# Fused attention and feed-forward kernel: similarities first, one-hot in steps 2 to 5, value products three key tiles every third step

## The chip, the cores and the metric

The kernel runs on one core of a Trainium2 chip. The core has a matrix engine (TensorE, PE in the profile; its weight loads are listed as PEld), VectorE (DVE), ScalarE (ACT), GpSimd (POOL), and a queue for DMAs (SyncE, SP). The metric is device time in microseconds, the median of several executions; one further execution is profiled.

## What is computed

Three stages, one after the other; the change lies in the first.

```python
# attention, for each batch b (2) and head h (8), 768 rows of 64
q_assign = argmax(q_n @ c_n.T)          # the nearest of 16 centroids of the head
k_assign = argmax(k_n @ c_n.T)
scores = q @ k.T / 8, and -1e9 where q_assign != k_assign
attn = softmax(scores) @ v
# mixing over the rows, then a feed-forward block (512 -> 2048 -> 512)
u = x + (x.T @ U @ V).T
x = u + relu(u @ w_ch1) @ w_ch2
# gated block with a convolution of three rows
h = relu(x @ w_in); gate = sigmoid(conv3(h)); out = (h * gate) @ w_out
```

## The kernel before

**Tiles and steps.** Queries go in tiles of 128 rows, six to a head, 16 heads, so 96 *steps* n (function `step`, L654). Two heads of a batch are a *pair*; there are eight pairs, 0 to 7, of 12 steps each, and s is the step within the pair (`divmod(n, 2 * NT)`). All engines run their own instructions in the order in which the program issues them, so `step` is a schedule written by hand. A step n does, in this order on TensorE:

- `s_mm(n + 2)`: scores of the tile two steps ahead, four matmuls, two of L364 (which finish an earlier `s_mm_ab`) and two of L375. The query and key operands are split in a high and a low part (`ab`, `cd`), and the `cd` tile holds 16 extra rows with the one-hot of the cluster, large where query and key agree. The scores have two PSUM buffers (pool `ps_s`).
- `pv_mm`: value products of the head before (L418), in the steps and with the key tiles that `PLAN` (L651) gives. r counts the steps of a head, shifted by one, so r = 0, 2, 4 are s = 1, 3, 5, 7, 9, 11, two of the six key tiles in each. `fin_t` (L434) turns the finished head back, in s = 1 and 7.
- at times an item of `mixing`, in the steps `MIX_AT` (L652: 0, 4, 8, 10): `mix_t` (L572), six `mix_u` (L588), and `mix_x` (L600) of the first batch, from step 8 of pair 4 on.
- `sims_wide` (s = 2) and `sims_turn` (s = 3), see below.
- `t_mm(n)`: six transposes of the tile's exponentials (L402).

ScalarE and VectorE take what falls due: `t_out(n - 1)` copies the transposed exponentials, one half on each (L409); `s_exp(n + 1)` is the exponential on ScalarE (L393); `s_max(n + 2)` is VectorE's maximum (L381), which the exponential needs. Then come `fin_x` (L440, L443), the evacuation of the mixing item, and `prep(n)` (L620).

**Side work of a pair.** While a pair runs, the next one is prepared: `sims_wide` (L226) multiplies centroids with queries and keys, `sims_copy` (L231, ScalarE) brings the result to SBUF, `sims_turn` (L240) transposes it into the PSUM tile `sim`, five parts on VectorE (`onehot_part`: L257 `mx`, L259 `eq`, L261 `eq` by an index, L263 `m2`, L265 `oh`) make the one-hot, parts 0 and 1 of which read `sim`; `onehot_t` (L273) transposes it, `onehot_rows` (L279, VectorE) scales it to `os`, and four DMAs on SP's queue (L287) put its rows into `cd`. In the pairs from 1 on the parts stand in steps 3, 3, 4, 4, 5 and the last two functions at the end of step 6. For pair 1, prepared during pair 0, there is a form of its own: `sims` (L215), 24 small matmuls ahead of and in step 0, with `warm` matmuls on zeros between them, parts in steps 0, 0, 1, 2, 3, and rows in step 5.

**Other queues.** `load_ops` (L113 to L115, issued by GpSimd) and `load_raw` (L96 to L98, SP) load a pair's operands; `split_ops` (L125, L126, GpSimd) makes the low parts: of the next pair's first head in step 1, of its second in step 7, when its loads have landed. `pump` (steps of odd n) moves the weight jobs on by one operation: with one job to a pair, VectorE's L473, L477 and L481 fall into s = 9, 11 and 1, ScalarE's L468 and L527 into s = 7 and 3.

**The rotating PSUM pool.** `ps_t` has three buffers, all under one tag: the two halves of the transposes of a step, `simw`, `sim`, `oht`, `at` and the mixing tiles take them in turn, so each waits until the tile three before it has been read.

Of the kernel before, what the change touches and what calls it, by code (L numbers as in the profile page):

```python
# [17 lines left out]
F32 = mybir.dt.float32  # L18
# [3 lines left out]
AF = mybir.ActivationFunctionType  # L22
ALU = mybir.AluOpType
# [3 lines left out]
P = 128  # L27
# [6 lines left out]
def tile_kernel(ctx: ExitStack, tc: tile.TileContext, qk, vv, cen, u_w, v_w, w1, w2, win, wout, conv, out):  # L34
    nc = tc.nc
    B, H, D, _, S = qk.shape
    NC = cen.shape[0] // H
# [167 lines left out]

    ohst = {}

    def sims(b, p, tiles=range(NT)):
        rq, rk = raw[b, p]
        if (b, p) not in ohst:  # L210
            ohst[b, p] = {"pm": ps_t.tile([P, NT * 4, NC], F32, tag="t", name="sim")}
        pm = ohst[b, p]["pm"]
        for t in tiles:
            for i, (r, cb) in enumerate(((rq, cbq), (rk, cbk))):
                nc.tensor.matmul(  # L215
                    pm[:, 4 * t + 2 * i:4 * t + 2 * i + 2, :].rearrange("p g c -> p (g c)"),
                    r[:, t * P:(t + 1) * P], cb[:, p], start=True, stop=True,
                )
# [47 lines left out]

    def onehot_t(b, p):
        oh = ohst[b, p]["oh"]
        pair = b * NP + p
        pt = ps_t.tile([4 * NC, S], BF16, tag="t", name="oht")  # L270
        for t in range(NT):
            g0 = 4 * t if pair == 1 else 8 * (t % (NT // 2)) + 4 * (t // (NT // 2))
            nc.tensor.transpose(pt[:, t * P:(t + 1) * P], oh[:, g0:g0 + 4].rearrange("p g c -> p (g c)"), identb)  # L273
        ohst[b, p]["pt"] = pt

    def onehot_rows(b, p):
        pt = ohst.pop((b, p))["pt"]
        os_ = a_oh.tile([4 * NC, S], F32R, tag="os", name="os")
        nc.vector.tensor_scalar(out=os_, in0=pt, scalar1=ohs[:, 0:1], scalar2=ohs[:, 1:2], op0=ALU.mult, op1=ALU.add)  # L279
        put_rows(b, p, os_, range(2))  # L280

    def put_rows(b, p, os_, heads):
# [337 lines left out]
    def prep(n):  # L620

        pair, s = divmod(n, 2 * NT)
        nxt = pair + 1
        if nxt < B * NP:
            b, p = divmod(nxt, NP)
            for part, at in enumerate((3, 3, 4, 4, 5) if nxt > 1 else (0, 0, 1, 2, 3)):
                if s == at and (nxt > 1 or part > 1):
                    sims_onehot(b, p, part)
            if s == 1:
                split_ops(b, p, 0, nc.gpsimd)  # L630
            elif s == 3:
                load_ops(b, p, 1)
            elif s == 7:
                split_ops(b, p, 1, nc.gpsimd)
            elif s == 8:
                load_v(b, p)
            if s == (6 if nxt > 1 else 5):
                onehot_t(b, p)
                onehot_rows(b, p)
        if s == 10 and pair + 2 < B * NP:  # L640
            load_raw(*divmod(pair + 2, NP))
            load_ops(*divmod(pair + 2, NP), 0)
        if n == NQ - 7:
            queue_chunk(1, lambda: wpc)
        if n >= NQ - 7:
            pump(FLOW)
        elif n % 2 == 1 and n > 1:
            pump(THIN)


    PLAN = ({2 * k: (2 * k, 2 * k + 1) for k in range(NK)}, NT - 2), ({k: (2 * k, 2 * k + 1) for k in range(NK)}, NK - 1)  # L651
    MIX_AT = (0, 4, 8, 10)  # L652

    def step(n):  # L654
        pair, s = divmod(n, 2 * NT)
# [4 lines left out]
                mixing.append(mix_t(b))  # L660
                mix_rest(b)
        if n == 0:

            for t in range(2, NT):
                sims(0, 1, (t,))
                warm(1)
        if n + 2 < NQ:
            s_mm(n + 2)

        g, r = divmod(n - NT - 1, NT)  # L670
        ks, last = PLAN[g == NHEAD - 1]
# [6 lines left out]
        elif mixing and (s in MIX_AT or pair == B * NP - 1):  # L678
            mix = mixing.pop(0)
            got = mix[0]()  # L680
        if s == 2 and n < NQ and 1 < pair + 1 < B * NP:
            sims_wide(*divmod(pair + 1, NP))
        if s == 3 and n < NQ and 1 < pair + 1 < B * NP:
            sims_turn(*divmod(pair + 1, NP))
        if 0 <= n < NQ:
            t_mm(n)
        if 0 <= n - 1 < NQ:
# [283 lines left out]
```

## Time and profile before

| | us |
|---|---|
| median of 3 runs | 667.9 (667.74 to 668.18) |
| the profiled execution, device time | 668.33 |
| its span in the profile | 666.3 |
| granted TensorE clock over the span | 1.0 of full speed |

A row of a timeline has the start in us from the span's start, the duration, the engine, the line of the kernel, the operation, and out<-in with partitions x elements; x8 at its end means eight such instructions merged, and the bracket tells the idle time of the engine just before it and what released it. Matmuls are pipelined, so the time from one start to the next is what one costs.

### The profile page before, as it was taken

What the parts mean: (1) busy time and instruction counts of PE and PEld (TensorE: products, weight loads), DVE (VectorE), ACT (ScalarE), POOL (GpSimd) and SP (SyncE); (2) the same over time, 40 slices, a digit from 0 to 9 for tenths busy, and PEclk for the clock granted to TensorE, in tenths of its full rate; (3) what the DMA queues carried; (4) which work ended last, traced back from release to release, by engine and by line L of the source; (5) the groups of instructions that cost most, each with busy time, mean ns of one, the idle gap of its engine ahead of it and who ended that gap; (6) DMA issues with size and microseconds to landing.
All of it is one profiled execution on the core that took longest, in us unless ns stands there. A gap on an engine that the chain in (4) does not pass through costs nothing.

```text
span 666.3 us, 9744 instructions
## 1 busy us (share of the span) xinstructions
PE 648.6 (97%) x3660; PEld 511.5 (77%) x3660; DVE 428.1 (64%) x744; ACT 319.9 (48%) x613; POOL 221.3 (33%) x222
## 2 busy tenths in 40 slices
PE   8999999999999999999999999999999999999997
PEld 6766766666676766789888888888877888888886
DVE  6988788887889875388326868873177445643400
ACT  5765666666666773334213343331135367753511
POOL 3844436252434013046331333331055634321300
PEclk9999999999999999999999999999999999999999
DMA  7765655727273202022102343330013000000111
GB/s 184 147 147 129 140 128 117 173 61 174 60 174 70 91 29 98 1 95 96 65 0 95 105 148 127 126 127 32 1 64 126 1 1 0 3 31 24 41 47 48
DMA packets 19583, 55.45 MB, mean 83 GB/s; under 512 B 3312, under 2 KB 7024, under 8 KB 19536
## 3 DMA queue, kind: packets, MB, share of 16 engines
q1 hardware_dynamic: 15936, 40.08, 20.1%
q0 software_dynamic: 3600, 14.75, 10.9%
q8 instruction: 29, 0.48, 0.3%
q14 instruction: 18, 0.15, 0.1%
HBM read 50.19 MB, written 3.15 MB: 80 GB/s over the span
## 4 chain that ended last, share of the span: by engine, by line
PE 82%; DVE 10%; issue 3%; ACT 2%; POOL 1%; DMA 0%; DVEq 0%; ACTq 0%; POOLq 0%
PE g L860 10%; PE pv L418 9%; PE tr L402 7%; PE h L737 6%; PE h L739 6%; PE h L738 6%; PE a L753 6%; PE a L755 5%; PE a L754 5%; PE sc L364 4%; PE sc L375 4%; PE po L894 3%; PE po L895 3%; PE po L896 3%; DVE e L381 2%
## 5 line engine op out<-in xcount | busy, mean ns | idle before, releaser
L528 POOL TENSOR_TENSOR wl<-wx,wh 128x512 fp32r<-128x512 f32 x48 | 63.1, 1316 | 143.9 <-ACT wh L527 137.9
L393 ACT ACTIVATE e<-sc,nb 128x768 f32<-128x768 f32 x96 | 86.8, 905 | 21.8 <-DVE e L381 21.5
L381 DVE TENSOR_SCALAR_CACHE_REDUCE e<-sc 128x768 f32<-128x768 f32 x96 | 91.3, 952 | 7.2 <-PE sc L375 6.7
L743 DVE SCALAR_TENSOR_TENSOR rl<-h,rh 128x512 fp32r<-128x512 f32 (+1 forms) x52 | 33.7, 647 | 85.8 <-ACT rh L742 85.8
L742 ACT ACTIVATE rh<-h 128x512 fp32r<-128x512 f32 (+1 forms) x52 | 29.3, 563 | 113.1 <-PE h L739 113.1
L402 PEld LDWEIGHTS tr<-identf,e 128*128 128x128 f32 x576 | 65.2, 140 | 23.3 <-issue 5.0
L402 PE MATMUL tr<-identf,e 128*128 128x128 f32 x576 | 81.2, 276 | 1.2 <-ACT tt L581 0.7
L737 PE MATMUL h<-uh,wh 128*128 128x512 f32 (+1 forms) x208 | 78.3, 376 | 1.6 <-DVE rl L743 1.6
L753 PE MATMUL a<-rh,wh 128*128 128x512 f32 (+1 forms) x208 | 78.3, 376 | 0.5 <-DVE xa L769 0.5
L754 PE MATMUL a<-rl,wh 128*128 128x512 f32 (+1 forms) x208 | 77.7, 374 | 0.3 <-DVE rl L743 0.3
L738 PE MATMUL h<-ul,wh 128*128 128x512 f32 (+1 forms) x208 | 77.6, 373 | 0.0
L739 PE MATMUL h<-uh,wl 128*128 128x512 f32 (+1 forms) x208 | 77.5, 373 | 0.0
L755 PE MATMUL a<-rh,wl 128*128 128x512 f32 (+1 forms) x208 | 77.5, 373 | 0.0
L418 PE MATMUL pv<-pt,rv 128*64 128x384 f32 x384 | 72.5, 499 | 0.0
L409 ACT COPY pt<-tr 128x384 f32<-128x384 f32 x96 | 46.0, 479 | 41.1 <-PE tr L402 41.0
L409 DVE COPY pt<-tr 128x384 f32<-128x384 f32 x96 | 52.8, 551 | 14.3 <-PE tr L402 13.6
L364 PE MATMUL sc<-ab 128*128 128x384 f32 x192 | 57.5, 381 | 2.0 <-POOL ab L126 0.8
L527 ACT CAST wh<-wx 128x512 fp32r<-128x512 f32 x48 | 29.7, 619 | 59.8 <-DVE wx L481 59.8
L477 DVE SCALAR_TENSOR_TENSOR wx<-wb,wx 128x512 int32<-128x512 int32 (+3 forms) x52 | 47.9, 921 | 11.6 <-ACT wb L468 9.6
L877 POOL TENSOR_TENSOR h<-h,cv 128x768 f32<-128x768 f32 x16 | 29.6, 1849 | 64.8 <-ACT cv L876 64.8
L375 PE MATMUL sc<-cd 80*128 80x384 f32 x192 | 49.5, 339 | 0.0
L737 PEld LDWEIGHTS h<-uh,wh 128*128 128x128 f32 x208 | 39.2, 188 | 9.3 <-DVE rl L743 1.9
(139 smaller groups left out, 1261.3 us busy)
## 6 DMA issues: line engine op xcount, KB each, us to landing
raw<-in_w_dram SPq DMA_DIRECT2D x32, 512.0 KB, 3.5
cd<-in_qk_dram POOLq DMA_DIRECT2D x15, 384.0 KB, 4.3
ab<-in_qk_dram POOLq DMA_DIRECT2D x15, 384.0 KB, 5.4
raw<-in_win_dram SPq DMA_DIRECT2D x8, 512.0 KB, 3.5
raw<-in_wout_dram SPq DMA_DIRECT2D x8, 512.0 KB, 3.5
rv<-in_vv_dram SPq DMA_DIRECT2D x8, 384.0 KB, 3.3
out_dram<-o SPq DMA_DIRECT2D x24, 128.0 KB, 1.8
ab<-in_qk_dram POOLq DMA_DIRECT2D x15, 192.0 KB, 5.7
```

The source lines that it names most:

```text
L364: nc.tensor.matmul(ps[:, f, 0:HS], ab[:, 0, c0:c0 + P], ab[:, 1, f * HS:(f + 1) * HS], start=True, stop=False)
L381: nc.vector.tensor_scalar(out=e, in0=ps[:, :, 0:HS], scalar1=-SCALE, scalar2=3e38, op0=ALU.mult, op1=ALU.min, accum_out=nb,)
L393: nc.scalar.activation(e, ps[:, :, 0:HS], AF.Exp, scale=SCALE, bias=nb, accum_out=st["sum", n // NT][:, n % NT:n % NT + 1])
L402: nc.tensor.transpose(pt[:, k, :], e[:, i, k * P:(k + 1) * P], identf)
L409: (nc.scalar.copy if i == 0 else nc.vector.tensor_copy)(to, st.pop(("t", n, i)))
L418: nc.tensor.matmul(acc[i * D:(i + 1) * D], vts[b, h // 2][:, h % 2, k], pt[:, k, i * NK:(i + 1) * NK].rearrange("p a b -> p (a b)"), start ...
L737: nc.tensor.matmul(ph, wh[:, k, ws], uh[g][:, k, ts], start=(k == 0), stop=False)
L738: nc.tensor.matmul(ph, wh[:, k, ws], ul[g][:, k, ts], start=False, stop=False)
L739: nc.tensor.matmul(ph, wl[:, k, ws], uh[g][:, k, ts], start=False, stop=(k == ND - 1))
L753: nc.tensor.matmul(accs[d][:, 0:n], wh[:, i, ds_], rh, start=(f == 0), stop=False)
L754: nc.tensor.matmul(accs[d][:, 0:n], wh[:, i, ds_], rl, start=False, stop=False)
L755: nc.tensor.matmul(accs[d][:, 0:n], wl[:, i, ds_], rh, start=False, stop=(f == NH - 1))
```

## The change

- `PLAN`: the value products of a head come three key tiles at a time, in r = 0 and r = 3, that is s = 1, 4, 7, 10 (the last head keeps its plan); the head's accumulator is copied out after r = 3 and not after r = 4. `MIX_AT` becomes 3, 6, 8, 9, 11.
- Side work from pair 1 on: `sims_wide` and `sims_copy` in step 0, `sims_turn` in step 2, the five parts in steps 2, 2, 3, 3, 4, `onehot_t` in step 5 right behind the scores and ahead of any value products, and `onehot_rows` in step 5 behind the exponential. `onehot_rows` runs on ScalarE, an activation with function Identity and pointer scale and bias, in place of VectorE's `tensor_scalar`.
- Pair 0: `sims` is removed. `sims_wide` stands at the head of step 0, with `warm(7)` behind it (four `warm` matmuls stand where the first `sims` were), `sims_turn` in step 4, the parts in steps 4, 4, 5, 5, 6, `onehot_t` and `onehot_rows` in step 7.
- Ahead of step 0, GpSimd makes the split of head 1 before it issues the loads for pair 1's first head, and not after.

```diff
-    def sims(b, p, tiles=range(NT)):
...
     def onehot_t(b, p):
...
-            g0 = 4 * t if pair == 1 else 8 * (t % (NT // 2)) + 4 * (t // (NT // 2))
+            g0 = 8 * (t % (NT // 2)) + 4 * (t // (NT // 2))
...
     def onehot_rows(b, p):
...
-        nc.vector.tensor_scalar(out=os_, in0=pt, scalar1=ohs[:, 0:1], scalar2=ohs[:, 1:2], op0=ALU.mult, op1=ALU.add)
+        nc.scalar.activation(os_, pt, AF.Identity, scale=ohs[:, 0:1], bias=ohs[:, 1:2])
...
     first_pair()
-    sims(0, 1, range(2))
+    warm(4)
...
-            for part, at in enumerate((3, 3, 4, 4, 5) if nxt > 1 else (0, 0, 1, 2, 3)):
-                if s == at and (nxt > 1 or part > 1):
+            for part, at in enumerate(ONEHOT_AT[nxt == 1]):
+                if s == at:
                     sims_onehot(b, p, part)
...
-            if s == (6 if nxt > 1 else 5):
-                onehot_t(b, p)
-                onehot_rows(b, p)
...
-    PLAN = ({2 * k: (2 * k, 2 * k + 1) for k in range(NK)}, NT - 2), ({k: (2 * k, 2 * k + 1) for k in range(NK)}, NK - 1)
-    MIX_AT = (0, 4, 8, 10)
+    PLAN = ({0: (0, 1, 2), NK: (3, 4, 5)}, NK), ({k: (2 * k, 2 * k + 1) for k in range(NK)}, NK - 1)
+    MIX_AT = (3, 6, 8, 9, 11)
+
+    SIM_AT, TURN_AT, ONEHOT_AT, ROWS_AT = 0, (2, 4), ((2, 2, 3, 3, 4), (4, 4, 5, 5, 6)), (5, 7)
...
         if n == 0:
-            for t in range(2, NT):
-                sims(0, 1, (t,))
-                warm(1)
+            sims_wide(0, 1)
+            warm(7)
         if n + 2 < NQ:
             s_mm(n + 2)
+        ahead = divmod(pair + 1, NP)
+        wide = 0 <= n < NQ and 1 < pair + 1 < B * NP
+        rows = 0 <= n < NQ and pair + 1 < B * NP and s == ROWS_AT[pair == 0]
+        turn = 0 <= n < NQ and pair + 1 < B * NP and s == TURN_AT[pair == 0]
+        if rows:
+            onehot_t(*ahead)
...
-        if s == 2 and n < NQ and 1 < pair + 1 < B * NP:
-            sims_wide(*divmod(pair + 1, NP))
-        if s == 3 and n < NQ and 1 < pair + 1 < B * NP:
-            sims_turn(*divmod(pair + 1, NP))
+        if s == SIM_AT and wide:
+            sims_wide(*ahead)
+        if turn:
+            sims_turn(*ahead)
...
-        if s == 2 and n < NQ and 1 < pair + 1 < B * NP:
-            sims_copy(*divmod(pair + 1, NP))
+        if rows:
+            onehot_rows(*ahead)
+        if (s == SIM_AT and wide) or n == 0:
+            sims_copy(*ahead)
         if n == -1:
             split_first(1, "q")
+            split_ops(0, 0, 1, nc.gpsimd)
             load_ops(0, 1, 0)
-            split_ops(0, 0, 1, nc.gpsimd)
-        if n == 0:
-            sims_onehot(0, 1, 0)
-            sims_onehot(0, 1, 1)
```

## Rows read from the trace of the kernel before

**Rows 1.** The page of the profile: busy time and share of the span of each engine

```profile
PE 648.6 (97%) x3660; PEld 511.5 (77%) x3660; DVE 428.1 (64%) x744; ACT 319.9 (48%) x613; POOL 221.3 (33%) x222
```

**Rows 2.** Stretch 80 to 110 us: busy us (count) of PE, PEld, DVE, ACT, POOL

```profile
80.00:110.00 30.00, 29.06 (x197) 20.47 (x196) 24.59 (x50) 19.12 (x41) 12.86 (x15) 1.00 0.62 133
```

**Rows 3.** Waits of 14 to 300 us: line <- releaser: us, times, longest

```profile
PE oht L273 <- DVE pt L409: 5.5, 6, 0.9
```

**Rows 4.** Timeline of TensorE over two steps: start us, us, operation

```profile
96.15 0.52 PE L375 MATMUL sc<-cd 80*128 80x384 f32 x2
...
97.56 0.51 PE L375 MATMUL sc<-cd 80*128 80x384 f32 x2
...
98.00 1.51 PE L418 MATMUL pv<-pt,rv 128*64 128x384 f32 x8
...
99.44 0.88 PE L402 MATMUL tr<-identf,e 128*128 128x128 f32 x6
...
100.50 0.51 PE L375 MATMUL sc<-cd 80*128 80x384 f32 x2
```

**Rows 5.** Timeline, TensorE's weight loads within a burst of value products

```profile
132.28 0.14 PEld L418 LDWEIGHTS pv<-pt,rv 128*64 128x64 f32 x2 [0.18 <-issue]
...
132.61 0.14 PEld L418 LDWEIGHTS pv<-pt,rv 128*64 128x64 f32 x2 [0.18 <-issue]
```

**Rows 6.** Timeline, steps 5 and 6 of a pair on TensorE, VectorE and GpSimd

```profile
112.36 0.35 DVE L261 TENSOR_TENSOR eq<-eq,iota 128x384 bf16<-128x384 bf16 x1
...
114.46 1.82 POOL L126 TENSOR_TENSOR ab<-rq,ab 64x768 fp32r<-64x768 f32 x1
...
114.55 2.15 DVE L265 TENSOR_TENSOR oh<-eq,m 128x384 bf16<-128x384 bf16 x1
...
115.11 0.51 PE L375 MATMUL sc<-cd 80*128 80x384 f32 x2
...
117.22 0.49 PE L273 MATMUL oht<-identb,oh 128*64 128x128 bf16 x6 [0.94 <-DVE pt L409]
...
118.09 0.52 PE L375 MATMUL sc<-cd 80*128 80x384 f32 x2
```

**Rows 7.** Timeline near the start, two steps without value products

```profile
18.54 0.52 PE L375 MATMUL sc<-cd 80*128 80x384 f32 x2
...
19.18 0.96 DVE L381 TENSOR_SCALAR_CACHE_REDUCE e<-sc 128x768 f32<-128x768 f32 x1 [0.37 <-PE sc L375]
...
20.18 0.90 ACT L393 ACTIVATE e<-sc,nb 128x768 f32<-128x768 f32 x1 [0.28 <-DVE e L381]
...
21.67 0.52 PE L375 MATMUL sc<-cd 80*128 80x384 f32 x2
```

**Rows 8.** Timeline, the similarities turned in two pairs, and read

```profile
79.79 0.55 PE L240 MATMUL sim<-identf,sw 128*128 128x128 f32 x3
...
109.37 0.55 PE L240 MATMUL sim<-identf,sw 128*128 128x128 f32 x3
...
109.95 0.56 DVE L257 TENSOR_REDUCE mx<-sim 128x24 f32<-128x384 f32 x1 [0.87 <-PE sim L240]
```

**Rows 9.** Timeline, the weight job's L481 in two pairs, and a GpSimd split

```profile
104.85 0.54 DVE L481 SCALAR_TENSOR_TENSOR wx<-wb,wx 96x384 int32<-96x384 int32 x1
...
134.15 1.82 POOL L126 TENSOR_TENSOR ab<-rk,ab 64x768 fp32r<-64x768 f32 x1 [2.05 <-DMA raw<-in_w_dram]
...
134.41 2.11 DVE L481 SCALAR_TENSOR_TENSOR wx<-wb,wx 128x512 int32<-128x512 int32 x1
```

**Rows 10.** Groups by line (count | busy us, mean ns | idle): VectorE, ScalarE

```profile
L279 DVE TENSOR_SCALAR os<-oht,ohs 64x768 fp32r<-64x768 bf16 x7 | 7.4, 1064 | 0.0
...
L869 ACT ACTIVATE cv<-h,cw 128x768 f32<-128x768 f32 x16 | 15.0, 938 | 0.5
...
L876 ACT ACT_TABLE_LOAD x1 | 1.3, 1283 | 2.3 <-DVE cv L871 2.3
```

**Rows 11.** Timeline, step 9's exponential in the pair with mixing

```profile
157.62 0.91 ACT L393 ACTIVATE e<-sc,nb 128x768 f32<-128x768 f32 x1
```

More of the change, by code (lines that the diff above doesn't have):

```diff
@@ L206, in tile_kernel @@
     ohst = {}
-    def sims(b, p, tiles=range(NT)):
[L209 to L218, printed above, removed]
     def sims_wide(b, p):
@@ L268, in onehot_t @@
         oh = ohst[b, p]["oh"]
-        pair = b * NP + p
         pt = ps_t.tile([4 * NC, S], BF16, tag="t", name="oht")
         for t in range(NT):
-            g0 = 4 * t if pair == 1 else 8 * (t % (NT // 2)) + 4 * (t // (NT // 2))
+            g0 = 8 * (t % (NT // 2)) + 4 * (t // (NT // 2))
             nc.tensor.transpose(pt[:, t * P:(t + 1) * P], oh[:, g0:g0 + 4].rearrange("p g c -> p (g c)"), identb)
```

## The prediction

> **What bounds the kernel now.** I read the page's busy times first: TensorE is busy 648.6 of 666.3 us [rows 1]. So time can come only from work or waits on TensorE, and the change leaves nearly all of its work. Its parts lie in the attention stage, the first 250 us, so I read a stretch of that stage next: of 30 us TensorE has 29.06, VectorE 24.59, ScalarE 19.12 [rows 2]. VectorE is second and not far off, which matters as soon as TensorE's long steps are dealt out otherwise. The only wait of TensorE that comes back in each pair is that of the one-hot transposes L273, 5.5 us in 6 waits [rows 3].
>
> Then I took the stage step by step, from one L375 to the next [rows 4]. A step without value products takes 97.56 - 96.15 = 1.41 us, one with two key tiles 100.50 - 97.56 = 2.94. Two steps are 4.35, and ScalarE and VectorE catch up in each long one. A burst runs from 98.00 to 99.44, 1.44; its weight loads for a half tile come 0.33 apart [rows 5], so a key tile more is 0.65, and some 0.1 of a burst is fixed.
>
> Where the wait arises [rows 6]: `oh` started at 114.55 beside GpSimd's L126, which runs from 114.46 to 116.28, and took 2.15, while another bf16 operation of that size took 0.35 before GpSimd began. The transposes of step 6 then start at 117.22 with 0.94 idle before them, and the step is 118.09 - 115.11 = 2.98. Without it: 1.41 + 0.49 = 1.90. The loss is 1.08.
>
> **The change part by part** (against the profiled execution, 668.33 us, of which the span is 666.3; the median of the runs is 0.4 lower). Plus is slower.
>
> (a) Value products: per head three bursts of two tiles become two of three. 3 x 4.35 = 13.05 before; 2 x (2.94 + 0.65) + 4 x 1.41 = 12.82 after. -0.23 for 15 heads (the last keeps its plan): -3.4.
>
> (b) `oh` moves from step 5 to step 4, so it should be over before GpSimd's split of the pair's second head begins. The wait of 1.08 goes, in six pairs: -6.5. What is late next is the subject of (d) to (f).
>
> (c) The turning of the similarities (step 2) and the one-hot transposes (step 5, now ahead of the step's own) stand in short steps, as bursts of their own: 2 x 6 x 0.1 = +1.0, an estimate from the fixed part of a burst.
>
> (d) Two short steps in a row. The scores have two buffers, so the scores of step n wait for the exponential of the tile two before. The trace has this once, near the start, where there are no value products yet [rows 7]: L375 at 18.54, VectorE's maximum 19.18, ScalarE's exponential 20.18, the next L375 on that buffer 21.67. The round takes 3.13, two short steps 2.82: +0.31. A long step between hid it all along; now each head has two such gaps. They stand open in steps 8-9 of pairs 0 to 3 and 7, and twice more in pair 7, which prepares no next pair: 7 x 0.31 = +2.2. Steps 11-0 are covered by the similarities' own eight matmuls, now in step 0. It is 0 where mixing fills the step; pairs 5 and 6 are so counted.
>
> (e) Steps 2-3. The turned similarities hold one of three rotating PSUM buffers until `mx` and `eq` have read them; the third tile after them is the first transpose of step 3. From step 2's L375: maximum after 0.64 and busy 0.95 [rows 7], `mx` 0.56 [rows 8], `eq` of the same size as long, some 0.1 to release: 2.8. TensorE would be there after a short step, the turning (0.4 and the 0.1 of (c)) and the step's own scores (0.4): 2.3, where 0.4 is the lead from 97.56 to 98.00 [rows 4]. Wait 0.5, six pairs: +3.0. Before, this lay behind the value products of step 3. On top, the weight job's L481 of step 1 is queued on VectorE ahead of step 2's copy and maximum, and now starts 0.65 later, after the longer burst. It took 0.54 beside an idle GpSimd (at 384 columns) and 2.11 beside the split (at 512) [rows 9]. At 0.54 it pushes the maximum by some 0.15, at 2.11 by some 0.9. I take two of six blocked: 4 x 0.15 + 2 x 0.9 = 2.4; bounds 0.9 (none) and 5.4 (all). Before already lost about 1.0 to the same cause, most of it in the pair of rows 9. Together +4.4.
>
> (f) `os` goes from VectorE (1064 ns) to ScalarE, which the trace of before doesn't show. The nearest rows have the same 768 columns: 0.90, the exponential [rows 7], and 0.94, L869, the same function with a pointer scale [rows 10]; I take 0.9. It stands in step 5 ahead of step 6's copy and exponential, on the round of (d): step 7's scores wait some 0.5. Four pairs 0.5, pair 5 0.3 and pair 6 0.1 (mixing fills step 6): +2.4; bounds 1.0 (half the wait) and 3.0. The four row DMAs go out about a step earlier on SP's queue, and the raw loads behind them too; that pays for moving the similarities, which read raw, from step 2 to 0, and I cost both at nothing. If that cover is gone, step 0 waits for a load, up to 1 us a pair by my estimate.
>
> L279 took 1064 ns on VectorE and reads PSUM [rows 10]. The Trainium skill, "ScalarE: Activation LUTs", section Rules for kernel authors, speaks against the move: it wants multiplications and additions on VectorE, up to three times as fast there in bf16. By that `os` would take some 3.2 us on ScalarE (an estimate from that factor and L279) and the sum would be +16 in place of +2.6; L869's 0.94 speaks against it.
>
> (g) Mixing, pair 4. `mix_t` stays in step 8, its evacuation, a chain of twelve small operations, keeps ScalarE from step 9's exponential until 157.62 [rows 11]; the first `mix_u`, which reads its result, moves from step 10 to 9, and step 9 has no value products to hide it. TensorE reaches step 10 as late as now (that exponential sets it), with one key tile fewer done, and steps 10 and 11 then cost 3.59 + 1.41 and not 1.41 + 2.94, +0.65; with the 0.65 that step 7 takes longer, and not the -0.23 of (a), it is some +1.3 (the mixing item that pair 4 has more is one less later); bounds 0.5 and 2.2.
>
> (h) Pair 0. Its next pair's one-hot work moves from steps 0 to 3 to steps 4 to 6, short ones, its transposes ahead of step 7's value products. VectorE must, from the maximum of step 4 on, do three maxima (0.95 [rows 7]), two copies (half the size, some 0.5 by estimate) and five parts (0.56 twice [rows 8]; 0.35 to 2.15 [rows 6] each for three, of which I let one or none meet a split): 6.0 to 7.5, and begins 0.64 behind TensorE's L375 [rows 7]. TensorE gets to the transposes after 3 x 1.41 + 0.5 + 0.4 = 5.1 and the waits of some 0.9 that it meets on the way as in (d) and (e). So they wait 0.6 to 2.1. I take 1.5, since GpSimd's split of the next pair's first head, whose loads go out after the split for head 1 now, falls into these steps; less some 0.3 that the steps 0 to 3 gain, which are rid of that work: +1.2; bounds 0 and 1.8. The split for head 1 is earlier on GpSimd's queue, which I leave to the lower bound; the loads behind it are first read for scores in step 10. The warm-up matmuls trade places with the first similarities while TensorE waits for the first exponentials: 0.
>
> Sum: -3.4 - 6.5 + 1.0 + 2.2 + 4.4 + 2.4 + 1.3 + 1.2 = +2.6. 668.3 + 2.6 - 0.4 = **670.5 us**, its own range 669.3 to 674.
>
> **The rivals.** *Faster: VectorE isn't late.* The same work in total, 1 us a pair less on VectorE, and 5.4 of 30 us idle there [rows 2]: if the similarities' buffer is free within 2.2 us of step 2's L375 and not 2.8, (e) is 0, (h) 0 and (f) half: 2.6 - 4.4 - 1.2 - 1.2 = -4.2, 663.7. For it: the chain of (e) is short of its mark by only half a us. Against it: each link is a row.
>
> *No change.* L481 never meets the split (-1.9) and pair 0 stays near its low end (-0.7): 668.
>
> *Much slower: a long `os`.* If the function of `os` needed a table load and the next exponential another, 1.28 us each [rows 10], they would lie on the round of step 6: 7 x 2.56 = 18, 688. If `os` took three times L279's 1.06 us, 2.3 more than I take, in six pairs, 14: 684. That is what the rule named above would do. Against both: L869 takes 0.94, and the stage of L869 has a single load for its 16 uses [rows 10]; beside the exponential no row shows that function.
>
> **How the numbers follow.** A measurement of this kernel tells 0.2%, 1.3 us, from no change. Forecast 0.48, faster 0.26, no change 0.24, and 0.01 for each of the two long forms of `os`. Slower is the first and the last two, 0.50. The range runs from the faster rival, 664, to the upper bounds of (e) and (h) (3.0 and 0.6 more) with half the way to those of (f) and (g) (0.3 and 0.5): 2.6 + 4.4 = +7, 675; cases of both signs lie in it.
>
> **What would show it.** L375 to L375: 3.6 in steps 1, 4, 7, 10; step 6 below 2.4 and no wait of L273 for VectorE from pair 1 on, or (b) is wrong; steps 8 and 9 together 3.13 (d); first transpose of step 3 waiting for VectorE's `eq` (e); step 7's L364 waiting for ScalarE's exponential right behind `os` (f); transposes of step 7 of pair 0 waiting for `oh` over 0.5 (h). Pairs 1 to 3 should take 29.6 to 30.8 us each, from one L240 to the next, against 109.37 - 79.79 = 29.58 now [rows 8]. If they take under 29, the forecast is wrong at (e) or (f); a table load after the first two means the last rival.

## The result and the profile after

The changed kernel is slower: 674.27 us (671.48 to 675.37, 5 executions) against 667.74 (666.17 to 668.18, 5) for the kernel before in the same session, a ratio of 1.0099 with the interval 1.0075 to 1.0123. The forecast was 670.5 and slower. Sign and range held, but the loss is more than twice the predicted one. One execution of e5, the profiled one, took 916.62 us at a granted clock of 0.65 and stands in no number below; e11 repeats that kernel for its profile.

The profiled execution took 675.37 us, span 673.6. In the new kernel's lines L375 is L362, L364 is L351, L402 is L389, L418 is L405, L273 is L260, L279 is L266, L477 and L481 are L464 and L468, L588 is L575; L381, L393 and L409 are L368, L380 and L396, L226 is L214, L240 is L228, L257 to L265 are L245 to L253, L528 (GpSimd's part of a weight job) is L515. L568 ends the chain behind `mix_t`, L579 and L597 evacuate mixing items.

First the engine busy line of the page after, which answers to [rows 1]:

```profile
PE 651.9 (97%) x3654; PEld 512.5 (76%) x3654; DVE 416.3 (62%) x737; ACT 325.3 (48%) x621; POOL 221.4 (33%) x222
```

VectorE has 11.8 us less work, ScalarE 5.4 more, TensorE 3.3 more. No engine changed its rank, so the loss has to be looked for in waits. In the timelines I take one step as the time from a step's first L362 (before: L375) to the next, in us, summed by pair:

| pair | 0 | 1 | 2 | 3 | 4 | 5 | 6 | 7 | sum |
|---|---|---|---|---|---|---|---|---|---|
| before | 24.62 | 29.67 | 29.58 | 29.57 | 33.61 | 30.53 | 31.00 | 19.84 | 228.42 |
| after | 26.14 | 29.33 | 30.26 | 29.10 | 35.75 | 31.75 | 31.44 | 20.97 | 234.74 |

The steps lose 6.3; the first of them begins 1.15 later (17.78 against 16.63), behind a stretch of 3.4 us near the start at a lower granted clock. Together that is, within 0.2, the 7.3 us by which the span grew; from the last scores on the two traces run alike. I don't put the late start down to the change: in every experiment with the new start but e5 the first step begins at 16.0 to 16.3. Pairs 1 and 3 did gain. Pairs 0, 2 and 4 to 7 lost. Pair 3, step by step:

| s | 0 | 1 | 2 | 3 | 4 | 5 | 6 | 7 | 8 | 9 | 10 | 11 |
|---|---|---|---|---|---|---|---|---|---|---|---|---|
| before | 1.41 | 3.28 | 2.29 | 3.29 | 1.40 | 2.95 | 2.98 | 3.28 | 1.39 | 2.95 | 1.41 | 2.94 |
| after | 2.29 | 3.92 | 1.69 | 1.77 | 3.61 | 1.96 | 1.78 | 3.93 | 1.40 | 1.77 | 3.59 | 1.41 |

Step 6 has lost its wait ([rows 6]). But steps 3, 6 and 9, each a short step behind another, take 1.77 and not 1.41. These waits in the timeline of the kernel after, pair 3:

```profile
110.08 0.49 PE L228 MATMUL sim<-identf,sw 128*128 128x128 f32 x3
...
111.24 0.55 DVE L245 TENSOR_REDUCE mx<-sim 128x24 f32<-128x384 f32 x1
...
111.83 0.56 DVE L247 TENSOR_TENSOR eq<-sim,mx 128x384 bf16<-128x384 f32 x1
...
112.45 0.55 PE L389 MATMUL tr<-identf,e 128*128 128x128 f32 x3 [0.19 <-DVE eq L247]
...
117.79 0.99 ACT L266 ACTIVATE os<-oht,ohs 64x768 fp32r<-64x768 bf16 x1
...
120.08 0.61 PE L351 MATMUL sc<-ab 128*128 128x384 f32 x2 [0.16 <-ACT e L380]
...
124.46 0.52 PE L362 MATMUL sc<-cd 80*128 80x384 f32 x2
...
126.10 0.90 ACT L380 ACTIVATE e<-sc,nb 128x768 f32<-128x768 f32 x1 [0.28 <-DVE e L368]
...
127.19 0.59 PE L351 MATMUL sc<-ab 128*128 128x384 f32 x2 [0.16 <-issue]
...
127.62 0.51 PE L362 MATMUL sc<-cd 80*128 80x384 f32 x2
```

The first is step 3's transposes behind `eq`, the reader of `sim`; the second is step 7's scores behind the exponential that stood behind `os`. The third is step 9's round of scores, maximum and exponential: the scores at 127.19 use the buffer that the exponential read until 127.00, and from L362 to L362 the round takes 127.62 - 124.46 = 3.16, in two steps that would take 2.82. Each bracket is short because the weight loads ahead of it waited too; the step lengths give the whole price, 0.36.

**Pair 2** lost 1.16 in step 0. VectorE and GpSimd there:

```profile
73.21 1.82 POOL L126 TENSOR_TENSOR ab<-rk,ab 64x768 fp32r<-64x768 f32 x1
...
73.37 2.07 DVE L464 SCALAR_TENSOR_TENSOR wx<-wb,wx 96x384 int32<-96x384 int32 x1
...
75.97 0.55 PE L389 MATMUL tr<-identf,e 128*128 128x128 f32 x3 [0.94 <-DVE pt L396]
```

In pair 3 the same L464 ran before the split and took 0.55. Here it lasts until just after the split's end (75.03), and the copy that TensorE needs is queued behind it. **Pair 5**, step 5:

```profile
178.76 0.68 DVE L579 TENSOR_TENSOR x<-x,mu 128x512 f32<-128x512 f32 x1
...
178.96 1.27 POOL L515 TENSOR_TENSOR wl<-wx,wh 128x512 fp32r<-128x512 f32 x1
...
179.36 1.08 DVE L249 TENSOR_TENSOR eq<-eq,iota 128x384 bf16<-128x384 bf16 x1
...
181.74 1.82 POOL L125 TENSOR_TENSOR ab<-rk,cd 64x768 fp32r<-64x768 f32 x1 [1.19 <-DMA cd<-in_qk_dram]
...
182.29 1.68 DVE L253 TENSOR_TENSOR oh<-eq,m 128x384 bf16<-128x384 bf16 x1
...
184.03 0.52 PE L260 MATMUL oht<-identb,oh 128*64 128x128 bf16 x6 [1.15 <-DVE oh L253]
```

Step 3's mixing addition L579 stands ahead of the one-hot parts and pushes them back by 0.60; so `eq` comes to lie beside GpSimd's L515 and takes 1.08 where it takes 0.35 in e10, and `oh` meets the split after all. The wait that the change removed is back, a step earlier. **Pair 4**, where `mix_u` now follows `mix_t` by one step; the timeline, then the stretches (busy of PE, PEld, DVE, ACT, POOL, then the granted clock):

```profile
159.71 0.26 ACT L568 CAST tt<-mt 32x128 fp32r<-32x128 f32 x1 [0.36 <-DVE tt L567]
...
160.01 0.51 PE L575 MATMUL mu<-tt,v 96*128 96x512 f32 x1 [2.11 <-ACT tt L568]
```

```profile
157.60:160.90 3.30, 1.19 (x8) 0.77 (x7) 2.06 (x5) 2.20 (x7) 1.63 (x3) 0.99 0.74 194
160.90:164.30 3.40, 3.32 (x11) 1.76 (x11) 2.60 (x7) 1.72 (x5) 1.44 (x2) 0.50 0.92 172
```

TensorE waits 2.11 and then works 3.4 us at a granted clock of 0.50, the 1.2 GHz level; step 10 takes 4.53 and not 3.59. **Pair 0**:

```profile
30.61 0.55 DVE L253 TENSOR_TENSOR oh<-eq,m 128x384 bf16<-128x384 bf16 x1
...
31.22 0.47 PE L260 MATMUL oht<-identb,oh 128*64 128x128 bf16 x5 [0.67 <-DVE oh L253]
...
38.85 0.59 PE L362 MATMUL sc<-cd 80*128 80x384 f32 x2 [0.86 <-DMA cd<-os]
```

The transposes wait for `oh`, as forecast, and the scores of step 10 wait for the row DMA that goes out two steps later than before.

### The profile page after: what moved, and what is told of

Read it like the earlier page. It is cut to its first block, busy times and chain, and to the rows that moved or that the text cites. A ratio compares the mean times of both kernels' runs of the same rounds, so it can differ in the third digit from the quotient of the medians.

```text
span 673.6 us, 9731 instructions
## 1 busy us (share of the span) xinstructions
PE 651.9 (97%) x3654; PEld 512.5 (76%) x3654; DVE 416.3 (62%) x737; ACT 325.3 (48%) x621; POOL 221.4 (33%) x222
## 4 chain that ended last, share of the span: by engine, by line
PE 79%; DVE 10%; ACT 4%; issue 3%; DMA 1%; POOL 1%; ACTq 0%; SPq 0%; DVEq 0%; POOLq 0%
PE g L849 10%; PE pv L405 9%; PE tr L389 6%; PE h L726 6%; PE h L728 6%; PE h L727 6%; PE a L742 5%; PE a L744 5%; PE a L743 5%; PE sc L351 4%; PE sc L362 3%; PE po L883 3%; PE po L884 3%; PE po L885 3%; DVE e L368 2%
## 5 line engine op out<-in xcount | busy, mean ns | idle before, releaser
L515 POOL TENSOR_TENSOR wl<-wx,wh 128x512 fp32r<-128x512 f32 x48 | 62.9, 1313 | 145.4 <-ACT wh L514 139.4
L368 DVE TENSOR_SCALAR_CACHE_REDUCE e<-sc 128x768 f32<-128x768 f32 x96 | 91.4, 953 | 12.8 <-PE sc L362 11.1
L380 ACT ACTIVATE e<-sc,nb 128x768 f32<-128x768 f32 x96 | 86.8, 904 | 14.4 <-DVE e L368 13.8
L389 PE MATMUL tr<-identf,e 128*128 128x128 f32 x576 | 83.2, 277 | 3.6 <-DVE pt L396 1.8
L389 PEld LDWEIGHTS tr<-identf,e 128*128 128x128 f32 x576 | 65.1, 140 | 23.4 <-issue 7.4
L405 PE MATMUL pv<-pt,rv 128*64 128x384 f32 x384 | 69.9, 498 | 0.0
L396 DVE COPY pt<-tr 128x384 f32<-128x384 f32 x96 | 53.0, 552 | 19.6 <-PE tr L389 18.6
L396 ACT COPY pt<-tr 128x384 f32<-128x384 f32 x96 | 45.6, 476 | 35.0 <-PE tr L389 35.0
L351 PE MATMUL sc<-ab 128*128 128x384 f32 x192 | 58.4, 387 | 2.7 <-ACT e L380 1.5
L464 DVE SCALAR_TENSOR_TENSOR wx<-wb,wx 128x512 int32<-128x512 int32 (+3 forms) x52 | 50.0, 962 | 11.5 <-ACT wb L455 9.4
L866 POOL TENSOR_TENSOR h<-h,cv 128x768 f32<-128x768 f32 x16 | 29.6, 1851 | 64.8 <-ACT cv L865 64.8
L362 PE MATMUL sc<-cd 80*128 80x384 f32 x192 | 49.8, 342 | 0.9 <-DMA cd<-os 0.9
L405 PEld LDWEIGHTS pv<-pt,rv 128*64 128x64 f32 x384 | 25.1, 137 | 31.0 <-issue 30.5
```

The lines of the kernel that those rows point to most:

```text
L351: nc.tensor.matmul(ps[:, f, 0:HS], ab[:, 0, c0:c0 + P], ab[:, 1, f * HS:(f + 1) * HS], start=True, stop=False)
L368: nc.vector.tensor_scalar(out=e, in0=ps[:, :, 0:HS], scalar1=-SCALE, scalar2=3e38, op0=ALU.mult, op1=ALU.min, accum_out=nb,)
L380: nc.scalar.activation(e, ps[:, :, 0:HS], AF.Exp, scale=SCALE, bias=nb, accum_out=st["sum", n // NT][:, n % NT:n % NT + 1])
L389: nc.tensor.transpose(pt[:, k, :], e[:, i, k * P:(k + 1) * P], identf)
L396: (nc.scalar.copy if i == 0 else nc.vector.tensor_copy)(to, st.pop(("t", n, i)))
L405: nc.tensor.matmul(acc[i * D:(i + 1) * D], vts[b, h // 2][:, h % 2, k], pt[:, k, i * NK:(i + 1) * NK].rearrange("p a b -> p (a b)"), start ...
```

## The experiments

"Before" took 666.48 to 666.88 in these sessions; each ratio is to it. Step sums by pair of the kernels that decide (from their timelines, as above):

| pair | 0 | 1 | 2 | 3 | 4 | 5 | 6 | 7 | sum |
|---|---|---|---|---|---|---|---|---|---|
| e1 | 25.12 | 28.50 | 28.51 | 28.51 | 31.87 | 30.13 | 33.72 | 19.86 | 226.22 |
| e2 | 24.69 | 29.02 | 28.93 | 28.97 | 34.45 | 32.49 | 31.33 | 20.98 | 230.87 |
| e6 | 24.33 | 28.59 | 28.59 | 28.59 | 31.87 | 29.37 | 29.96 | 19.84 | 221.16 |
| e9 | 25.45 | 29.83 | 28.51 | 28.51 | 32.14 | 29.44 | 30.19 | 19.60 | 223.65 |
| e10 | 25.73 | 29.70 | 29.11 | 29.10 | 37.01 | 29.85 | 31.02 | 20.85 | 232.37 |
| e11 | 25.02 | 35.13 | 29.09 | 29.09 | 35.41 | 30.58 | 29.97 | 20.94 | 235.23 |

**e1: the moved side work without the plan.**

```diff
-    PLAN = ({0: (0, 1, 2), NK: (3, 4, 5)}, NK), ...
-    MIX_AT = (3, 6, 8, 9, 11)
+    PLAN = ({2 * k: (2 * k, 2 * k + 1) for k in range(NK)}, NT - 2), ...
+    MIX_AT = (0, 4, 8, 10)
```

> The changed kernel with the old PLAN (two key tiles in r = 0, 2, 4) and the old MIX_AT (0, 4, 8, 10); the side work stays in its new steps. Theory A (the loss is the short steps two in a row, in which waits stand open): every wait of the changed kernel's pairs 1 to 4 goes, a pair takes about 28.5 us (6 x 4.35 + 0.68 + 0.89 + 0.29 + 0.5), pair 0 about 25.0; the kernel takes 660 to 662.5, faster than both. Theory B (the side work's new steps are the loss: similarities in step 0, `os` on ScalarE, pair 0 late): 668 to 672.

664.72 us, ratio 0.9969 (0.9957 to 0.9981): faster than both kernels. Pairs 1 to 3 take 28.5, 1.1 less than before, so the side work's move by itself is a gain of the size of one wait of [rows 6]. Pairs 0 to 3 came as theory A had them, the time (660 to 662.5) did not, because of pairs 5 and 6, where a mixing operation of step 4 stands ahead of `oh`. Pair 6 of e1:

```profile
201.20 0.69 DVE L597 TENSOR_TENSOR ul<-mx,uh 128x512 fp32r<-128x512 f32 x1
201.72 1.79 POOL L125 TENSOR_TENSOR ab<-rk,cd 64x768 fp32r<-64x768 f32 x1 [0.90 <-DMA cd<-in_qk_dram]
201.81 2.12 DVE L253 TENSOR_TENSOR oh<-eq,m 128x384 bf16<-128x384 bf16 x1
...
203.98 0.47 PE L260 MATMUL oht<-identb,oh 128*64 128x128 bf16 x5 [2.08 <-DVE oh L253]
```

**e2: the plan without the side work.** The kernel before with the new `PLAN` and `MIX_AT`.

```diff
-    PLAN = ({2 * k: (2 * k, 2 * k + 1) for k in range(NK)}, NT - 2), ...
-    MIX_AT = (0, 4, 8, 10)
+    PLAN = ({0: (0, 1, 2), NK: (3, 4, 5)}, NK), ...
+    MIX_AT = (3, 6, 8, 9, 11)
```

> The kernel before with the new PLAN and the new MIX_AT only. Theory A: steps 8-9 and 11-0 of each pair take 3.1 to 3.2 together, step 6 keeps its wait for `oh`, pairs 1 to 3 take about 30.4; 671 to 675. Theory B: the plan alone saves the fixed parts of its bursts, 3.4 us: 663 to 666.

670.38 us, ratio 1.0054 (1.0042 to 1.0066): slower, near the 671 of theory A, but pairs 1 to 3 gain 0.6 each, which neither theory had. With the old side work step 6 falls to 2.1 to 2.3 there. So both halves of the change take away the same wait, and their gains don't add. The loss of e2 is in pairs 4, 5 and 7.

**e3: the first `mix_t` in step 9, its reader in step 11.**

```diff
-    MIX_AT = (3, 6, 8, 9, 11)
+    MIX_AT = (3, 6, 9, 11)
```

> The changed kernel with MIX_AT = (3, 6, 9, 11): the first mixing item of pair 4 moves from step 8 to 9, so that its evacuation lies beside the value products of step 10, and no mixing item reads it before step 11. Theory G (the evacuation stood open in step 9 and cost 1.9 us, and 0.9 more where the clock fell behind the wait): steps 8 to 11 of pair 4 take 11 to 11.5 and not 13.9, the granted clock stays 1.0 there, 671 to 672.5. Rival: the chain is as long wherever it stands, 674 +- 0.7.

671.21 us, ratio 1.0066 (1.0054 to 1.0078), against 1.0099, some 2 us less than the changed kernel. Steps 8 to 11 of pair 4 take 10.46 and not 13.93, and the granted clock stays at 1.00 over the span. Part comes back in pairs 5 and 7 (32.60 and 21.65 against 31.75 and 20.97): in pair 7 an item that was pushed on stands in step 0 (2.36 and not 1.74), and in step 0 of pair 5 (3.85) L464 met a split. The wait of 2.11 in pair 4 and its clock were real.

**e4: `os` back on VectorE, in its new place.**

```diff
-        nc.scalar.activation(os_, pt, AF.Identity, scale=ohs[:, 0:1], bias=ohs[:, 1:2])
+        nc.vector.tensor_scalar(out=os_, in0=pt, scalar1=ohs[:, 0:1], scalar2=ohs[:, 1:2], op0=ALU.mult, op1=ALU.add)
```

> The changed kernel with `os` back on VectorE, in step 5. Theory F: the wait behind `os` only changes its engine: step 6's first transpose waits for the PSUM buffer that `os` reads until VectorE, behind step 5's maximum, has read it; step 6 takes 1.75 to 1.95, 674 +- 1. Rival (ScalarE's round alone is the wait): step 6 takes 1.4, some 2.2 us less in six pairs, 671 to 672.5.

677.28 us, ratio 1.0165 (1.0150 to 1.0179). Both expectations missed: step 6 rose from 1.78 to 2.52 in pairs 1 to 6. Ahead of step 7's scores TensorE now waits 0.89 where after it was 0.16. In e4, pair 3:

```profile
119.67 0.62 PE L351 MATMUL sc<-ab 128*128 128x384 f32 x2 [0.89 <-ACT e L380]
```

`os` on VectorE delays the maxima by more than it delays the exponential on ScalarE, so the move to ScalarE saves 0.74 a pair in this plan, 4.4 us in six pairs. The operation itself, in the groups of the kernel after, and in the answer on the tile `os` of e4 (min/median/max in ns):

```profile
L266 ACT ACTIVATE os<-oht,ohs 64x768 fp32r<-64x768 bf16 x7 | 6.9, 989 | 2.7 <-PE oht L260 2.1
```

```profile
L266 DVE TENSOR_SCALAR os<-oht,ohs x7: 1067/1067/1070, 30.4 to 219.5; 64x768 fp32r<-64x768 bf16 x7
```

**e5 and e11: the changed kernel without GpSimd's splits.** e11 is the same kernel as e5, run again for its profile. The low parts' place is loaded with the whole operands, so these kernels leave work out; one load in three is then twice as large.

```diff
-        nc.gpsimd.dma_start(out=ab[0:D, 1 - j], in_=qk[b, h, :, 1 - j])
+        nc.gpsimd.dma_start(out=ab[0:D], in_=qk[b, h])
...
-            if s == 1:
-                split_ops(b, p, 0, nc.gpsimd)
-            elif s == 3:
+            if s == 3:
                 load_ops(b, p, 1)
-            elif s == 7:
-                split_ops(b, p, 1, nc.gpsimd)
```

> The changed kernel without GpSimd's splits for pairs 1 to 7 (they are left out, and the low parts are loaded whole instead; nothing else on GpSimd is heavy in this stage). Theory C (VectorE's SBUF operations are held while GpSimd splits, and that is what made step 0 of pairs 2, 4, 5, 6 and step 5 of pairs 5 and 6 long): step 0 takes 2.29 wherever no mixing stands, step 5 about 1.96 in all pairs, `oh` and the weight job's operations 0.7 at most; some 4.7 us less than the changed kernel, 668.5 to 670.5 where that has 674.3; steps 8-9 still 3.17. Rival (VectorE is late on its own): step 5 of pairs 5 and 6 stays over 2.8, 673 to 675.

> The changed kernel with the low parts of the weights of pairs 1 to 7 loaded whole and not split on GpSimd, once more, for its profile (the low parts are then not those of the reference). Theory C (VectorE held beside GpSimd's splits is what costs in pairs 2, 4, 5 and 6): pairs 1 to 3 take 29.1 us each with step 0 at 2.3, step 5 of pairs 5 and 6 1.9 to 2.3, and the last scores come by 249 us. Rival (the waits of the changed kernel are not the splits' doing): step 0 of some pair is still over 2.8 and step 5 of pairs 5 and 6 over 2.9, last scores at 251 to 253. If the steps are rid of the waits and the time is still 674, the loss must stand before the first scores, behind the last, or in stretches at the lower granted clock.

674.67 us (ratio 1.0115, 1.0096 to 1.0134) and 673.91: no gain, and my theory seemed to fall. The trace of e11 shows why it did not: the waits that I put down to the splits are gone (step 0 of pairs 2 and 4 is 2.29 and of pair 6 2.36, step 5 of pairs 5 and 6 1.99), but one new wait has come, in step 0 of pair 1, which takes 8.13 and not 2.29:

```profile
46.09 0.60 PE L214 MATMUL simw<-rk,cbk 128*32 128x384 f32 x1 [3.62 <-DMA rk<-in_qk_dram]
```

The load that TensorE waits for is the second of `rk` (L98), issued at 35.82; it lands 10.1 us behind its issue, and none does so later than 6.1 in the kernel after. Without the split on its queue GpSimd issues its operand loads earlier, six in a row from 21.44 and the next from 35.28, beside those of `rk`, where after issues them from 38.26. Whether that or the larger load makes `rk` late I did not try. The wait is followed by another stretch at the lower clock. Less the 5.84 the steps would sum to 229.4, 5.3 less than after. Both expectations named one kind of wait; the transfer was in neither. That the splits cost the changed kernel so much rests on this subtraction, since no run of it has neither the splits nor the late load.

**e6: the kernel before without the splits.** The edit of e5.

> The kernel before without the same splits. Theory C: the wait of the one-hot transposes (1.08 in six pairs) goes, and the 1.0 of the weight job with it: step 6 about 1.9, 659 to 661 where the kernel before has 667; the gap between the two kernels without splits is then 8 to 10 us, all of it the changed plan's. Rival: no change.

661.02 us, ratio 0.9912 (0.9897 to 0.9927), as expected; here the similarities stand in step 2 and no load is late. The splits cost the kernel before 5.7 us by the times (7.3 in the step sums), the changed one some 5 by the subtraction above: they are a cost to both, and not more to the changed kernel, so they don't explain why it is the slower one.

**e7: pair 0's one-hot work earlier.**

```diff
-    SIM_AT, TURN_AT, ONEHOT_AT, ROWS_AT = 0, (2, 4), ((2, 2, 3, 3, 4), (4, 4, 5, 5, 6)), (5, 7)
+    SIM_AT, TURN_AT, ONEHOT_AT, ROWS_AT = 0, (2, 2), ((2, 2, 3, 3, 4), (2, 2, 3, 3, 4)), (5, 5)
```

> The changed kernel with pair 0's one-hot work in the same steps as that of the other pairs (turned in step 2, parts in 2, 2, 3, 3, 4, rows in step 5). Theory H (pair 0 lost 0.5 to 1.2 us to transposes that waited for `oh` in step 7, and up to 0.9 to rows that landed late for step 10's scores): pair 0 takes 24 to 24.5 and not 26.1, step 7 3.6, step 9 1.8; 1.5 to 2 us less than the changed kernel. Rival: 0 +- 0.5, since the early steps have no long one either.

673.45 us (670.92 to 676.55), ratio 1.0103 (1.0078 to 1.0127), not to be told from the changed kernel. Pair 0 took 27.55, more than the 26.14 of after: `oh` met the split of pair 1's first head, TensorE waited 1.74 for it, and its clock fell behind that wait.

```profile
25.21 1.80 POOL L125 TENSOR_TENSOR ab<-rq,cd 64x768 fp32r<-64x768 f32 x1 [2.91 <-DVE pt L396]
...
25.82 1.62 DVE L253 TENSOR_TENSOR oh<-eq,m 128x384 bf16<-128x384 bf16 x1
...
27.49 0.52 PE L260 MATMUL oht<-identb,oh 128*64 128x128 bf16 x6 [1.74 <-DVE oh L253]
```

**e8: a first try at a better kernel.** e1 with e7's pair 0 and mixing in steps 6, 8 and 10.

```diff
-    MIX_AT = (0, 4, 8, 10)
+    MIX_AT = (6, 8, 10)
```

> Old PLAN, side work in the new steps, pair 0 like the others, MIX_AT = (6, 8, 10), so that no mixing item of VectorE stands between the parts of the one-hot. Theory A and C together: pairs 1 to 3 28.5, pair 0 about 24.2, pairs 5 and 6 29.1 to 29.4 (step 5 at 3.5); 657.5 to 661, against 664.7 of the old plan with the old mixing steps. Rival (the long step 5 of pair 6 has another cause): pairs 5 and 6 stay at 30 to 33.7, 662 to 664.

663.82 us, ratio 0.9957 (0.9942 to 0.9971). Pairs 5 and 6 became clean (29.16 and 29.35), but pair 0 took 27.39 as in e7, and pair 7 21.35, since the mixing that found no step in pairs 5 and 6 was left for it (steps 0, 2 and 3). So the pairs are the theory's and the time is the rival's.

**e9 and e10: bursts of two against bursts of three, with the same mixing steps.** e9 is e1, e10 the changed kernel, each with

```diff
-    MIX_AT = ...
+    MIX_AT = (6, 8, 10, 11)
```

> The moved side work and os on ScalarE with the old bursts of two key tiles; mixing in steps 6, 8, 10 and 11, so that no mixing addition stands ahead of the one-hot parts of steps 2 to 4, and one-hot work of pair 0 in steps 4 to 7 as in the changed kernel. Theory (the losses that are left in pairs 5 and 6 come from mixing additions in steps 0 and 4 that push the one-hot parts into GpSimd's second split): pairs 5 and 6 take 29.2 to 29.6 us each (30.1 and 33.7 with mixing in steps 0 and 4), pair 0 25.1, pair 7 19.9, and the time is 660 to 662.5. Rival (the four mixing places are worth the same wherever they stand, a wait only moves): 663.5 to 665.

> The changed kernel with mixing in steps 6, 8, 10 and 11 in place of 3, 6, 8, 9 and 11: the first product that reads mix_t's result is again two steps after it, and no mixing addition stands ahead of the one-hot parts. Theory A (the change loses by where its mixing items stand, the bursts of three tiles cost little by themselves): pair 4 steps 8 to 11 within 12.5 us (13.9 now), steps 5 of pairs 5 and 6 at 2.0 (3.1 to 3.2 now), 668 to 670. Theory B (the bursts of three tiles, with two short steps in a row, are what loses): pairs 1 to 3 stay at 29.1 against 28.5 with bursts of two, pair 7 at 21, and the time stays at 671 to 674.

e9: 662.18 us, ratio **0.9925 (0.9909 to 0.9940)**, the fastest that computes all, as its theory had it, with pair 6 (30.19) a little over. In its pair 1 L468 met a split (step 2 is 2.89). e10: 671.40, ratio 1.0072 (1.0046 to 1.0098). They differ in `PLAN` alone, and that is 9.2 us, or 8.7 in the step sums: 0.6 in each of pairs 2 and 3, 1.2 in pairs 5 and 6 together, 1.25 in pair 7, and 4.9 in pair 4. Theory B holds; of theory A came true that step 5 of pairs 5 and 6 is back at 1.96. One pair of each (pair 2 of e9, pair 2 of e10), as in [rows 2]:

```profile
71.53:100.03 28.50, 28.29 (x192) 19.98 (x192) 22.19 (x50) 20.10 (x44) 10.21 (x12) 1.00 0.62 135
```

```profile
71.61:100.72 29.11, 28.60 (x193) 20.19 (x193) 22.15 (x49) 19.75 (x42) 12.11 (x14) 1.00 0.56 134
```

The pair is 0.6 longer, which is three waits of some 0.36 less what the bursts save: TensorE idles 0.2 us in the one and 0.5 in the other, and 0.3 more is counted as busy with one matmul more in the records. In pair 4 the transposes of step 9 wait for the chain of `mix_t`. In e9, whose step 9 has a burst of value products:

```profile
151.80 1.51 PE L405 MATMUL pv<-pt,rv 128*64 128x384 f32 x8
...
153.99 0.87 PE L389 MATMUL tr<-identf,e 128*128 128x128 f32 x6 [0.68 <-ACT tt L568]
```

In e10, whose step 9 has none, the wait, and the stretch behind it:

```profile
156.69 1.03 PE L389 MATMUL tr<-identf,e 128*128 128x128 f32 x6 [2.10 <-ACT tt L568]
```

```profile
157.30:164.10 6.80, 6.39 (x20) 2.80 (x19) 2.28 (x6) 2.26 (x6) 3.83 (x3) 0.50 0.55 101
```

The missing burst, 1.44 by [rows 4], is the difference of the waits, 2.10 - 0.68 = 1.42. Behind the longer one the clock falls, for 6.8 us, and step 10 takes 6.32, some 2.5 more than 3.6 and a `mix_u` of 0.2. These 2.5 are half of what pair 4 loses between e9 and e10.

**e12: e9 with pair 0's five parts in steps 2 and 3.**

```diff
-    SIM_AT, TURN_AT, ONEHOT_AT, ROWS_AT = 0, (2, 4), ((2, 2, 3, 3, 4), (4, 4, 5, 5, 6)), (5, 7)
+    SIM_AT, TURN_AT, ONEHOT_AT, ROWS_AT = 0, (2, 2), ((2, 2, 3, 3, 4), (2, 2, 3, 3, 3)), (5, 5)
```

> The kernel of e9 with pair 0's turning in step 2, its five one-hot parts in steps 2 and 3, and its transposes and rows in step 5: in e7 the last part met GpSimd's split of the next head, which began at 25.21, while the four parts before it were done by 24.56 us; here all five lie ahead of the split. Theory (the fault in e7 and e8 was this meeting, and the row DMAs that pair 0's step 10 waits for go out earlier): pair 0 takes 23.2 to 24.2 us (25.45 in e9), step 7 3.3 and step 9 1.45 there, and the time is 660 to 661.5. Rival (VectorE is so full in steps 2 and 3 that the copies are late and what is won in steps 7 and 9 is lost in 3 to 5): pair 0 at 25 to 26, 662 to 663.

662.87 us, ratio 0.9944 (0.9923 to 0.9965): no better than e9. Step 7 fell from 4.08 to 2.94 and step 9 from 3.32 to 2.94, but steps 2 to 6 took 1.76 more, so pair 0 is 25.65 against 25.45. `oh` took 0.56 and was done at 25.15 as the split began (25.10), so the meeting is gone, yet both numbers are the rival's; that a full VectorE is the reason is not shown.

**What the runs say together.** In step sums: before 228.42; side work moved, mixing placed well, bursts of two (e9) 223.65, -4.8; bursts of three in place of two (e10) 232.37, +8.7, of which some 2.5 is the stretch at the lower clock; the change's own mixing steps 234.74, +2.4. The sum is the +6.3 of the first table.

## Why the prediction was right or wrong

The sign was right, but the sum was too small: +2.6 for steps that lost 6.3. The terms, measured in the step tables as lengthenings of the steps named:

| term | predicted | measured | where |
|---|---|---|---|
| (a) bursts | -3.4 | -3.4 | a long step 3.59 to 3.61, as forecast |
| (b) wait gone | -6.5 | -3.6 | 5.9 to be had in step 6, by e6; back in pairs 5 (+1.2) and 6 (+1.1) |
| (c) short bursts | +1.0 | -0.6 | turning 0.28 in its own step, 0.34 before; transposes 0.55, and 0.59 in step 6 of e6 |
| (d) two short steps | +2.2 | +2.1 | 1.40 + 1.77 in pairs 1 to 3; three times 0.33 to 0.43 in pair 7 |
| (e) steps 2 and 3 | +4.4 | +4.2 | 2.6 in step 3 (pairs 5 and 6 by e10), 2.6 in step 0, less 1.0 in step 2 before |
| (f) `os` | +2.4 | +1.7 | 0.37 in step 6 of pairs 1 to 4, 0.2 in pair 5, none in pair 6 |
| (g) pair 4's mixing | +1.3 | +2.6 | 0.9 of it the clock |
| (h) pair 0 | +1.2 | +1.5 | 0.67 for `oh`, 0.86 for the row DMA |

The measured terms make 4.5. What remains, some 1.8 us of the 6.3, lies in pairs 5 and 7 for the most part, where the mixing items stand in other steps; I did not split it further. That (c) and (f) came 2.3 lower than forecast hid most of the 2.9 by which (b) missed. Pairs 1 to 3 took 29.33, 30.26 and 29.10, two of them better than the 29.6 to 30.8 of the forecast; the loss lies in the other pairs.

**(b) failed** at "it should be over before GpSimd's split of the pair's second head begins". I had counted only the parts' own steps. The change's mixing addition of step 3 is issued ahead of them on VectorE, in pairs 5 and 6 alone. e10, without an item in step 3, has 1.96 in both steps 5, and e11, without the split, 1.99: it takes both to bring the wait back. In pair 5 `oh` starts 0.84 ahead of the split in e10 and 0.55 behind it in after; of these 1.39 us L579 is 0.60 and the hold of `eq` beside L515 0.73. The size was off too: e6's step 6 without the wait takes 2.00 and not the 1.90 that I had added up, so the wait was worth 0.98 and not 1.08.

**(e) had the right sum for half the right reason.** The buffer held by `sim` cost 0.35 to 0.52 (0.36 in pair 3), near the 0.5. The blocked weight operation was not L481 in step 1, as I wrote: I had read it from [rows 9], where it was the one that met the split. After, the similarities in step 0 put 0.88 into that step, and it was L464, issued in step 11 and run at the start of step 0, that met the split of the next pair's first head. Which pairs meet is not fixed: step 0 is over 2.5 in pairs 2, 4 and 6 of after, 4 and 6 of e10, 3 and 6 of e7, 4 and 5 of e3, and 6 of e4, so that the sum came near the forecast is in part luck. In e9 L464 met the split before pairs 2 and 4 as well (1.48 and 1.95), in step 11 beside a burst, and step 0 stayed at 2.29.

**(g) was too small**, by the clock above all (0.9) and by step 9, 4.85 where it had been 4.48. I saw that step 9 would have no value products to hide the chain, and priced the work that moves, but not the longer wait. That wait did what no row of before shows: behind it TensorE ran at the lower level.

**(f) was right** in its mechanism and somewhat too large, 0.37 a pair and not 0.5. The rule of the Trainium skill ("ScalarE: Activation LUTs", section Rules for kernel authors), by which multiplications and additions belong on VectorE, does not hold for this operation, which reads PSUM and writes fp32r (the rule gives its factor for bf16): 0.99 us on ScalarE, 1.07 on VectorE, and e4, which has it there, is some 4 us slower than the changed kernel (1.0165 against 1.0099). No activation-table load was added either (three before and three after).

**(h)** came out by its waits, 0.67 for `oh`, within the 0.6 to 2.1 forecast (with one part held at 2.15 the upper end of its VectorE sum is 7.8 and not 7.5), but the row DMA that step 10 waited for, 0.86, was in no part of it.

**The rivals.** "VectorE isn't late" fell: the short second steps are on the round of scores, maximum and exponential, whatever VectorE has free. "No change" needed the weight operations to miss the split (L468 met it only once, but L464 took its place) and pair 0 at its low end. Both forms of a long `os` fell with 0.99. The cover that I named in (f), a raw load that comes in time for step 0, held in the changed kernel but is thin: in e11 it was gone, for 5.8 us and not the 1 that I estimated.

What I had missed as a whole is the price of the plan: I made (a) a gain and (d) to (g) side effects of several parts. By the step sums of e9 and e10 the same kernel stands at -4.8 with bursts of two and at +3.9 with bursts of three.

## What to carry to other kernels

A long burst on the busiest engine is also cover: count what each one hides before two are merged into one, since its removal opens the round of the short steps (0.36 each here) and every chain that lay beside it (`mix_t`, 0.68 to 2.10). When two edits each remove the same wait, measure each alone; here both gained in pairs 1 to 3, and the better kernel is the one with only the first. A step is placed by every operation queued ahead of it on its engine in every pair, not by those of the pair that was read.

## What the runs showed of the hardware

**VectorE beside a GpSimd split.** In five meetings an operation of VectorE that takes 0.55 by itself ended 0.41 to 0.43 us after the split of GpSimd beside it, whenever it had begun: L464 at 75.44 for a split that ended at 75.03, `oh` in pair 5 at 183.97 for 183.56, in e1 at 203.93 for 203.51, in e7 at 27.44 for 27.01; in [rows 6] 116.70 for 116.28. Longer and shorter ones fit: L481 of 512 columns, 0.68 by itself, ended 0.55 after its split (136.52 for 135.97 in [rows 9]), and `eq` of pair 5, 0.35 by itself, 0.21 after L515 (180.44 for 180.23). Each ends its own time, less some 0.13, behind GpSimd's, as if it began when that was done. These operations read two tiles in SBUF. Others were not touched; in pair 0 of the kernel after:

```profile
28.54 1.91 POOL L126 TENSOR_TENSOR ab<-rk,ab 64x768 fp32r<-64x768 f32 x1 [0.35 <-PE sc L362]
28.80 0.55 DVE L251 TENSOR_REDUCE m<-eq 128x24 bf16<-128x384 bf16 x1
29.27 0.55 DVE L396 COPY pt<-tr 128x384 f32<-128x384 f32 x1
```

The Trainium skill, "SBUF — State Buffer", section "SBUF: two separate sides", says that a VectorE operation with two SBUF inputs and a GpSimd operation that reads SBUF share a pair of ports, and that the one which comes second is blocked until the other's whole instruction is over. The trace agrees, with the 0.41 to 0.43 above, GpSimd having begun first each time; the reduction L251 has one SBUF input, the copy L396 reads PSUM.

**The clock behind a wait.** In the attention stage TensorE's granted clock was 0.50, the 1.2 GHz level, in stretches of 3.4 to 6.8 us. Each began between 0.1 us before and 1.4 us after the end of a wait of TensorE: of 2.10 to 2.21 us in pair 4 (after, e2, e4, e7, e10, e11), 2.08 in pair 6 of e1, 3.62 in pair 1 of e11, 1.74 and 1.65 in pair 0 of e7 and e8, 1.43 in pair 6 of e7, and 1.02 ahead of the first scores in after. It stayed at 1.00 behind 0.68 (e9), 1.15 (after, pair 5), 1.33 (e3, pair 5), 1.39 (e4, pair 6), and behind 1.02 ahead of the first scores in e8. The same wait of 1.02 is in both lists, so its length alone does not tell what follows. e3, e6, e9, e12 and the kernel before have no such stretch in this stage. In the changed kernel's executions the spread is 3.9 us, in e9's 1.2; I did not try which of these stretches come in each of them.
